# An attention and GEGLU kernel: first weights loaded by halves of their columns, and scores placed next to values in two chunks

## The chip, the cores and the metric

The kernel runs on one core of a Trainium2 chip. The metric is the device time of one execution in microseconds (us), median of several runs; "before" gave 348.88 us in three runs (348.76 to 349.36). The granted clock is the share of its full clock that TensorE was given; 0.50 is half clock. TensorE is PE in the profile, VectorE DVE, ScalarE ACT, GpSimd POOL, the queue of the sync engine SPq.

## The reference

```
batch, heads, seq, dim = 8, 8, 576, 64          # q, k, v float32
mask: heads 0-3: 0 <= i-j < 32;  heads 4-7: 0 <= i-j < 128 and (i-j) % 4 == 0
attn = softmax(q k^T / 8, masked);  x = attn v, reshaped to [4608, 512]
out  = (gelu(x @ w_gate) * (x @ w_val)) @ w_out  # w_gate, w_val [512,1536], w_out [1536,512]
```

## The kernel before

x is kept transposed in four slices of 128 features (`xT[0..3]`). The dense part runs in nine chunks of 512 tokens, each in 12 blocks of 128 hidden columns. A block is 4 gate and 4 value matmuls (one for each slice of xT), a Gelu on ScalarE and a product on VectorE. Four output blocks of 12 matmuls follow in each chunk, and the attention of later batches is put between these. The weights come in thirds of 512 hidden columns.

```
    def load_w(i):                                   # one third of both matrices
        cs = slice(i * CH, (i + 1) * CH)
        both = [nc.gpsimd.dma_start(out=t[i], in_=w[:, cs].rearrange("(kc p) n -> p kc n", p=P))
                for t, w in ((wg_t, moe_w_gate), (wv_t, moe_w_val))]
        gated(both[0])                               # waits for the load named in gate["dma"]
        return both
    ...
    gate["dma"] = gate_v                             # first piece of v of batch 0
    load_w(0)
    v_cast(0, sv0)
    ...
    w1 = load_w(1)[1]
    copy("pool", tiles["v", 0][1], r4(first_vd))     # cast of v, dilated heads
    ...                                              # attention of batch 0; xT[0], xT[1] finished
    load_w(2)                                        # on GpSimd, xT[2], xT[3] on VectorE
    gate["dma"] = w1                                 # q, k of batch 1 wait for the second third
    for t, src in ((0, q), (1, k)):
        gated(nc.sync.dma_start(out=st1[:, t], in_=sixes(src, 1)))
    qd1 = load_eights(1)
    wo1 = [load_wo(i) for i in range(3)][1]
    load_v_dil(1)
    ... cast_six("pool", q61, st1, t, hp)            # four casts, transposed by TensorE in block 10, 11
```

In chunk 0, blocks 0 and 1 are computed together, slice by slice (`ffn1_two`), so that TensorE can begin as soon as the first slice is ready. The places of the attention work are strings such as "3.6v": in output block 3 ahead of matmul 6, values. `s` is scores (TensorE, then the exponential on ScalarE), `v` values with their denominators, `x` the normalisation on VectorE, `m` the mask of an earlier score on VectorE, `w` the last values of the chunk, which use the scores' PSUM banks (pieces of `ps`, the memory into which the matmuls write). `P` is the exponentials.

The softmax here doesn't subtract the row's maximum and nothing guards it: scores larger than these inputs give would overflow.

Of the kernel before, what the change touches and what calls it, by code (L numbers as in the profile page):

```python
# [21 lines left out]
def kernel(  # L22
# [10 lines left out]
    nc = tc.nc  # L33
# [3 lines left out]
    P = 128  # L37
# [3 lines left out]
    CH = 512  # L41
# [31 lines left out]
    wg_t = [const.tile([P, NKC, CH], F16, tag=f"wg{i}", name=f"wg{i}") for i in range(3)]  # L73
    wv_t = [const.tile([P, NKC, CH], F16, tag=f"wv{i}", name=f"wv{i}") for i in range(3)]
# [61 lines left out]
    def load_w(i):  # L136
        cs = slice(i * CH, (i + 1) * CH)
        both = [
            nc.gpsimd.dma_start(out=t[i], in_=w[:, cs].rearrange("(kc p) n -> p kc n", p=P))
            for t, w in ((wg_t, moe_w_gate), (wv_t, moe_w_val))  # L140
        ]
        gated(both[0])
        return both

    def load_wo(i):
        return nc.gpsimd.dma_start(
            out=wo_t[i], in_=moe_w_out[i * CH : (i + 1) * CH, :].rearrange("(fc p) m -> p fc m", p=P)
        )
# [4 lines left out]
    def gated(ins):  # L153

        if "dma" in gate:
            tc.add_manual_dep(ins.ins, gate.pop("dma").ins.name, SYNC, reason="order of loads")
# [45 lines left out]
    def v_cast(b, sv):  # L202
        vp, vd, vt, vr = tiles["v", b]
        nc.gpsimd.tensor_copy(  # L204
            vp.rearrange("p j g x d -> p (j g) x d")[:, :, 0:3:2, :],
            sv[:, 0:4].rearrange("p j (g x) d -> p (j g) x d", x=2),
        )
        nc.gpsimd.tensor_copy(vt[:, :, 0:3:2, :], sv[:, 4].rearrange("p (g x) d -> p g x d", x=2))
# [468 lines left out]
        t_plain(0, q6, hp, 2 * hp, ("act", "dve"))  # L677
    nc.vector.tensor_scalar(bias_d, mask_d, 1.0, 60000.0, ALU.subtract, ALU.mult)
    gate["dma"] = gate_v
    load_w(0)  # L680
    v_cast(0, sv0)

    def r4(t):
# [21 lines left out]
    last_keys(0, 0, 2)  # L705
    last_keys(0, 2, HK, nc.gpsimd)
    w1 = load_w(1)[1]
    copy("pool", tiles["v", 0][1], r4(first_vd))

# [12 lines left out]


    load_w(2)
    gate["dma"] = w1
    st1 = ldp.tile([R6, 2, HK, 6 * D], F32, tag="st", name="st1")
# [8 lines left out]
    for hp in range(2):  # L735
# [16 lines left out]

    places = {
        1: "0.0m 1.3v 1.3s 1.3x 1.3m 2.5v 2.5s 2.5x 2.5m 3.0s 3.0m 3.6v 3.6x 3.12w",
        2: "0.0m 1.3v 1.3s 1.3x 1.3m 2.5v 2.5s 2.5x 2.5m 3.0s 3.0m 3.6v 3.6x 3.7s 3.12w 3.12m",
        3: "0.0m 1.3v 1.3s 1.3x 1.3m 2.5v 2.5s 2.5x 2.5m 2.11s 2.11m 3.4s 3.6v 3.6x 3.6m",
        4: "0.0m 1.3v 1.3s 1.3x 1.3m 2.4v 2.4s 2.4x 2.4m 2.11s 2.11m 3.7s 3.7m",
        5: "0.0m 1.3v 1.3s 1.3x 1.3m 2.1s 2.1m 2.10s 2.10m 3.6s 3.6m",
    }
# [2 lines left out]
    for c in range(NCH):  # L762
# [13 lines left out]
        for nb in range(NNB):  # L776
# [19 lines left out]
            if nb == NNB - 1 and c > 0 and s_list:  # L796
                n = s_list.pop(0)
# [130 lines left out]
```

## Time and profile before

| | before |
|---|---|
| time, median of 3 | 348.88 us |
| span of the profiled run | 347.3 us |
| TensorE busy | 335.7 us (97%) |
| VectorE, ScalarE, GpSimd busy | 58%, 43%, 24% |
| granted clock of TensorE | 1.00 |

A row of the order in time has the start, the length, the engine, the line and the operation, then in brackets the engine's idle time ahead of it and what ended that. A row of the chain has start, length and what the end of the kernel waited for at that time.

### The profile page before, as it was taken

To read this page: it belongs to the slowest core of one execution; us is meant where nothing else is said; L and a number is where in the kernel's file an instruction comes from. 1 tells how busy PE (TensorE), PEld (TensorE's weight loads), DVE (VectorE), ACT (ScalarE), POOL (GpSimd) and SP (SyncE) were. 2 spreads that over 40 slices of the span, in tenths; PEclk is the share of its full clock that TensorE was granted. 3 is DMA by queue.
4 is the path that set the end of the run, shared out by engine and by line. 5 is a ranking of instruction groups with operands and counts; after the bars stand their busy time and mean duration, and the time that the engine had idled before them with its cause. 6 is when DMAs were issued, how large, how long until landed. Compare 5 with 4: busy or idle time off the path is not lost.

```text
span 347.3 us, 6004 instructions
## 1 busy us (share of the span) xinstructions
PE 335.7 (97%) x2342; PEld 163.3 (47%) x2342; DVE 202.1 (58%) x309; ACT 147.9 (43%) x220; POOL 82.2 (24%) x121
## 2 busy tenths in 40 slices
PE   8879999999999999999999999999999999999996
PEld 3544454444544444444544454445444444444443
DVE  3874488543793369674778676975398423303320
ACT  1753473535543446336553547236623223323321
POOL 8693304630630630243006300420000000000000
PEclk9999999999999999999999999999999999999999
DMA  8999999999999993897169924891100020020002
GB/s 176 227 202 225 200 201 181 184 153 272 195 142 273 194 143 101 183 175 121 63 157 170 149 79 130 183 145 49 74 2 0 32 91 1 2 90 30 2 30 91
DMA packets 106460, 44.44 MB, mean 128 GB/s; under 512 B 83296, under 2 KB 101856, under 8 KB 106432
## 3 DMA queue, kind: packets, MB, share of 16 engines
q1 hardware_dynamic: 84192, 31.01, 40.7%
q0 software_dynamic: 21696, 12.33, 27.4%
q10 hardware_dynamic: 544, 0.72, 0.8%
q8 instruction: 18, 0.29, 0.4%
q14 instruction: 10, 0.08, 0.1%
HBM read 39.85 MB, written 9.44 MB: 142 GB/s over the span
## 4 chain that ended last, share of the span: by engine, by line
PE 71%; DVE 12%; DMA 10%; issue 3%; ACT 2%; POOL 1%; SPq 1%; DVEq 0%; POOLq 0%; ACTq 0%
PE ps L576 42%; PE ps L610 21%; PE ps L464 4%; DMA st<-in_k_dram 4%; DMA sv<-in_v_dram 3%; DMA wv<-in_moe_w_val_dram 3%; DVE dt L492 2%; DVE u_all L599 2%; DVE dt L525 2%; DVE rb L536 1%; DVE P L392 1%; DVE xT L551 1%; DVE xT L502 1%; PE ps L382 1%; PE ps L352 1%
## 5 line engine op out<-in xcount | busy, mean ns | idle before, releaser
L599 DVE SCALAR_TENSOR_TENSOR u_all<-g,ps 128x512 f16<-128x512 f16 x108 | 72.8, 684 | 76.3 <-PE ps L576 67.9
L598 ACT ACTIVATE g<-ps 128x512 f16<-128x512 f32 x108 | 63.9, 596 | 123.4 <-PE ps L576 122.9
L576 PE MATMUL ps<-xT,wg 128*128 128x512 f16 x432 | 114.0, 379 | 0.8 <-POOL xT L699 0.4
L576 PE MATMUL ps<-xT,wv 128*128 128x512 f16 x432 | 113.8, 379 | 0.8 <-DMA wv<-in_moe_w_val_dram 0.6
L610 PE MATMUL ps<-wo,u_all 128*128 128x512 f16 x420 | 97.2, 380 | 0.2 <-DVE qTd L295 0.2
L576 PEld LDWEIGHTS <-wv 128*128 128x128 f16 x432 | 42.3, 98 | 53.0 <-issue 1.6
L576 PEld LDWEIGHTS <-wg 128*128 128x128 f16 x432 | 41.3, 98 | 48.7 <-issue 1.1
L610 PEld LDWEIGHTS <-u_all 128*128 128x128 f16 x420 | 38.4, 98 | 44.4 <-issue 0.8
L621 ACT ACTIVATE osb<-ps 128x512 f32<-128x512 f32 x33 | 19.7, 598 | 40.0 <-PE ps L610 39.9
L220 POOL CAST qp<-st 128x2048 f16<-128x2048 f32 x6 | 11.4, 1893 | 103.5 <-DMA sv<-in_v_dram 59.0
L536 DVE STREAM_TRANSPOSE rb<-rc 128x576 f32<-128x576 f32 (+4 forms) x34 | 25.3, 743 | 1.3
L525 DVE STREAM_TRANSPOSE dt<-ps 128x576 f32<-128x576 f32 x21 | 16.3, 778 | 13.2 <-PE ps L464 13.0
L384 ACT ACTIVATE P<-ps 128x1152 f16<-128x1152 f32 x16 | 18.1, 1130 | 12.0 <-PE ps L382 12.0
L362 ACT ACTIVATE P<-ps 128x960 f16<-128x960 f32 x16 | 15.5, 970 | 10.4 <-PE ps L352 10.3
L551 DVE TENSOR_TENSOR xT<-ps,rb 128x576 f16<-128x576 f32 x16 | 17.9, 1131 | 2.2 <-PE ps L464 1.9
L392 DVE TENSOR_TENSOR P<-P,mask_d 128x1152 f16<-128x1152 f16 x13 | 9.8, 750 | 9.7 <-ACT P L384 9.7
L392 DVE TENSOR_TENSOR P<-P,mask_p 128x1344 f16<-128x1344 f16 x14 | 11.8, 856 | 2.9 <-ACT P L363 2.9
L464 PE MATMUL ps<-P,ones 128*64 128x96 f16 (+5 forms) x174 | 11.2, 244 | 2.2 <-DVE P L392 1.5
L464 PEld LDWEIGHTS <-ones 128*64 128x64 f16 x174 | 7.0, 109 | 11.6 <-issue 8.8
L623 DVE TENSOR_SCALAR osb<-ps 128x512 f32<-128x512 f32 x2 | 1.4, 691 | 18.2 <-PE ps L610 18.2
L204 POOL CAST vp<-sv 128x1024 f16<-128x1024 f32 x8 | 8.5, 1065 | 12.8 <-DMA sv<-in_v_dram 12.8
L492 DVE STREAM_TRANSPOSE dt<-ps 64x576 f32<-64x576 f32 x14 | 10.9, 781 | 0.4
(86 smaller groups left out, 247.0 us busy)
## 6 DMA issues: line engine op xcount, KB each, us to landing
out_dram<-osb SPq DMA_DIRECT2D x35, 256.0 KB, 2.0
sv<-in_v_dram SPq DMA_DIRECT2D x40, 128.0 KB, 3.5
st<-in_q_dram SPq DMA_DIRECT2D x24, 128.0 KB, 3.0
st<-in_k_dram SPq DMA_DIRECT2D x24, 128.0 KB, 3.7
vd<-in_v_dram POOLq DMA_DIRECT2D x7, 256.0 KB, 6.3
wg<-in_moe_w_gate_dram POOLq DMA_DIRECT2D x3, 512.0 KB, 7.4
wv<-in_moe_w_val_dram POOLq DMA_DIRECT2D x3, 512.0 KB, 10.3
wo<-in_moe_w_out_dram POOLq DMA_DIRECT2D x3, 512.0 KB, 20.0
```

What stands on the lines that cost most here:

```text
L384: nc.scalar.activation(pt, ps[:, b0 : b0 + 4, 0:DW], AF.Exp, bias=0.0, scale=scale)
L392: nc.vector.tensor_tensor(pt, pt, mb, ALU.mult)
L464: nc.tensor.matmul(o, lhs, rhs, start=st, stop=True, skip_group_check=True)
L492: nc.vector.transpose(dt[64 * hl : 64 * hl + 64].rearrange("p b c -> p (b c)"), both_rows(1 - hl, b0, hl))
L525: nc.vector.transpose(dst, den)
L536: nc.vector.transpose(rb[:, 0 : 32 * nb].rearrange("p (b c) -> p b c", c=32), bass.AP(tensor=rc.tensor, offset=rc.offset, ap=[rc.ap[0], [1 ...
L551: nc.vector.tensor_tensor(dst.rearrange("p (i m s) -> p i m s", m=2, s=2), num, rb.rearrange("p (s m i) -> p i m s", s=2, m=2), ALU.mult,)
L576: nc.tensor.matmul(ps[:, bank, :], w[:, kc, ns], xT[kc][:, tok], start=first, stop=end)
L598: nc.scalar.activation(g, ps[:, banks[0], :], AF.Gelu)
L599: nc.vector.scalar_tensor_tensor(u_all[:, nb, :], g, USCALE, ps[:, banks[1], :], ALU.mult, ALU.mult)
L610: nc.tensor.matmul(ps[:, bank, :], u_all[:, fc, tb * P : (tb + 1) * P], wo_t[fc // 4][:, fc % 4, :], start=(fc == 0), stop=(fc == NNB - 1),)
L621: nc.scalar.activation(osb, ps[:, bank, :], AF.Copy, bias=0.0, scale=1.0 / USCALE)
```

## The change

Its intent is twofold. TensorE waits for the first value weights at 21.2 us, while only the columns of blocks 0 and 1 are needed by then; halves, taken by turns, bring these sooner. And in chunks 2 and 3 one group of scores is moved directly behind a group of values, which saves a switch of the array's tiling.

```
+    def load_w_halves(i):
+        for half in range(2):
+            cs = slice(half * CH // 2, (half + 1) * CH // 2)
+            for t, w in ((wg_t, moe_w_gate), (wv_t, moe_w_val)):
+                src = w[:, i * CH : (i + 1) * CH][:, cs].rearrange("(kc p) n -> p kc n", p=P)
+                gated(nc.gpsimd.dma_start(out=t[i][:, :, cs], in_=src))
...
-    load_w(0)
+    load_w_halves(0)
...
-        2: "... 3.0s 3.0m 3.6v 3.6x 3.7s 3.12w 3.12m",
-        3: "... 2.11s 2.11m 3.4s 3.6v 3.6x 3.6m",
+        2: "... 3.0s 3.0m 3.6v 3.6s 3.6x 3.12w 3.12m",
+        3: "... 2.11s 2.11m 3.6v 3.6s 3.6x 3.6m",
```

## The prediction

> **What bounds the kernel now.** I read the page of the kernel before from its top: busy shares, then the chain of work that ended last, then the waits, and at last the order in time of the two stretches that the change touches.
>
> ```profile
> PE 335.7 (97%) x2342; PEld 163.3 (47%) x2342; DVE 202.1 (58%) x309; ACT 147.9 (43%) x220; POOL 82.2 (24%) x121
> ...
> PE ps L576 42%; PE ps L610 21%; PE ps L464 4%; DMA st<-in_k_dram 4%; DMA sv<-in_v_dram 3%; DMA wv<-in_moe_w_val_dram 3%; DVE dt L492 2%; DVE u_all L599 2%; DVE dt L525 2%; DVE rb L536 1%; DVE P L392 1%; DVE xT L551 1%; DVE xT L502 1%; PE ps L382 1%; PE ps L352 1%
> ```
>
> TensorE is busy 335.7 of 347.3 us, so only 11.6 us of its idle time exist to be won, and no single change of order can be worth per cents. But the chain also names three transfers: `sv` (v of the first batch), `wv` (value weights) and `st` (k of the second batch). In order of time, for the first 60 us, the chain reads:
>
> ```profile
> 3.70 11.39 DMA sv<-in_v_dram
> ...
> 16.98 0.68 POOL wg L139
> 17.65 9.21 DMA wv<-in_moe_w_val_dram
> ...
> 27.30 13.19 DMA st<-in_k_dram
> ...
> 40.54 0.83 POOL qp L293
> ```
>
> So up to 41.4 us the chain is a queue of loads: the second third of the weights (issued at 16.98) lands at 26.86, that landing lets the k of batch 1 be issued at 27.30, it lands at 40.48, GpSimd casts it, and only then can TensorE transpose it. The first third, which the change splits, travels on the same transfer engines ahead of that second third.
>
> TensorE's side of the start, from its order in time (start, length, then the idle time before and its releaser in brackets):
>
> ```profile
> 20.87 0.38 PE L576 MATMUL ps<-xT,wg 128*128 128x512 f16 x1 [0.37 <-POOL xT L699]
> 21.84 0.39 PE L576 MATMUL ps<-xT,wv 128*128 128x512 f16 x1 [0.59 <-DMA wv<-in_moe_w_val_dram]
> ...
> 24.34 0.38 PE L576 MATMUL ps<-xT,wg 128*128 128x512 f16 x1
> ...
> 41.42 0.43 PE L306 MATMUL ps<-ident,qp 96*128 96x96 f16 x6 [0.26 <-POOL qp L293]
> ```
>
> The 0.59 us is the wait that the halves are to remove. Two later lines matter more: at 24.34 TensorE has just been let go by VectorE's last normalisation (`norm_x`, two L551 instructions from 22.17 for 2.12 us, so to 24.29), and at 41.42 it waits for GpSimd's cast of the late k.
>
> The end of chunks 2 and 3:
>
> ```profile
> 133.24 0.49 PE L464 MATMUL ps<-P,ones 128*64 128x64 f16 x10 [0.22 <-DVE P L392]
> ...
> 134.28 0.47 PE L352 MATMUL ps<-qTp 64*128 64x160 f16 x10
> ...
> 136.18 0.49 PE L464 MATMUL ps<-P,ones 128*64 128x64 f16 x10 [0.25 <-ACT P L363]
> ...
> 171.08 0.77 PE L352 MATMUL ps<-qTp 64*128 64x160 f16 x10
> ```
>
> In chunk 2 the last values of the chunk (136.18) wait for the exponentials of scores issued at 134.28, because they reuse those PSUM banks. In chunk 3 the scores at 171.08 take 0.70 us until the next start where others take 0.40: ScalarE's previous exponential on the same banks ends only at 171.34.
>
> **What the Trainium skill says.** "DMA: Bandwidth & Descriptors", section "Why small descriptors are slow (HBM only)", gives every packet a fixed overhead and every transfer operation fixed metadata, so smaller pieces cost more per byte. The trace agrees: its records of single packets show weight packets of 1024 B taking 98 ns, and packets of 512 B (the later loads of q and k, `qd`, 256 values a row, the same shape as a half) taking 60 ns. Two of these for one of those is 120 against 98, 22% more. The same page, "Issuing engines are not separate DMA queues", says that loads from different engines end up on the same 16 transfer engines and interleave; the trace agrees, as the k load's packets and the weights' run mixed from 30 to 39 us, the weights' queue falling from about 200 packets a us to about 80. "TensorEngine Tiling (Array Packing)", section "Key Properties", says that changing the tiling mode drains TensorE. In the trace 14 full matmuls before a switch to values take 3.12 us (88.06 to 91.18), 14 x 0.216 = 3.02, so a switch out of full tiles costs 0.10; values followed directly by scores cost nothing extra (123.87 to 124.51 is 0.64; values followed by full matmuls, 172.31 to 172.96, 0.65).
>
> **Part 1, the halves.** No arithmetic changes and the bytes are the same. GpSimd issues four loads in place of two, 2 x 0.77 = 1.54 us more. From 12.29 to 15.25 it idles for `sv` (2.96 us), so these are hidden. First the gain: both first halves together are 1024 packets of 512 B; they should land by about 19.5 us, and columns 0 to 255 are all that blocks 0 and 1 read. So at 20.87 TensorE goes on to the value weights at once, and the 0.59 us vanish. But then the second slice of xT is ready only at about 22.17 (GpSimd, 19.39 + 2.78), the third at 23.24, the fourth at 24.29 (VectorE). TensorE is at 24.34 for the fourth slice in both kernels. Worth: about 0. Neither engine's chain starts from the weights.
>
> Now the cost. The first third is 2 x 128 x 4 = 1024 packets of 1024 B, in the halves 2048 of 512 B. Where only such packets run, the trace counts about 202 a us of 1024 B, and 308 to 310 a us of 512 B in the microseconds at 75 and 102, with 30 to 63 small ones beside; allowing for those, 325. That is 1024/202 = 5.1 us against 2048/325 = 6.3 us: **1.2 us more**. GpSimd's queue carries packets without a pause from 14 us to beyond 45 us, so everything behind moves by 1.2 us: the second third's landing from 26.86 to about 28.1, the issue of batch 1's q and k behind it, k's landing from 40.48 to about 41.7, the cast to 42.5, and the transposes that started at 41.42 to about 42.6. TensorE arrives there at 41.16 as before, so the whole 1.2 us is idle time on the path. The loads behind it (output weights, v of batch 1) move by the same 1.2 us as TensorE, so they neither help nor hurt. Part 1: **+1.2 us**.
>
> **Part 2, chunk 2.** The scores move ahead of one output matmul and adjoin the values, which end at 133.94. They start there in place of 134.28: one switch (0.10) and one matmul (0.22) earlier, so the exponentials end at 135.8 in place of 136.13. TensorE, with six output matmuls after the scores, arrives at 135.74; the last values start at 135.84 in place of 136.18. VectorE idles 0.34 us before its transposes at 137.09, so it can follow. **-0.34 us**.
>
> **Part 3, chunk 3.** The scores move behind the values, so they no longer meet the busy banks (0.30 saved) and one switch goes (0.10). But the values then arrive at 169.89 + 7 x 0.216 + 0.10 = 171.50, and their P is masked by VectorE only at 171.63 (0.75 from 170.88), so they start at 171.70: 0.20 lost again. Then 0.65 values, 0.40 scores, 6 x 0.216 = 1.30: the next chunk starts at 174.05 in place of 174.26. The exponentials now end at about 174.2 in place of 173.21; the first matmul of chunk 4 needs only the banks of the first exponential (free at 173.7), and the second group, at 174.70, those of the second. No new wait. **-0.21 us**.
>
> Sum: 1.2 - 0.34 - 0.21 = +0.65, so 348.88 + 0.65 = 349.5.
>
> **The rivals.** (a) The transfers do not delay anything: 512 B packets mixed with others flow as well per byte as 1024 B ones. Then only parts 2 and 3 count, 348.3. For it: the packets' 60 ns is a duration with overlap, not a rate. Against: the counted rates show the same ratio. (b) The halves bring the intended 0.59 us as well: 347.7. Against: xT sets 24.34, and k sets 41.42, where any earlier arrival would only wait. (c) In chunk 3 ScalarE becomes the bound: its exponentials, now 1 us later, hold the banks of chunk 4's first matmuls, up to 0.6 us, so 350.1. Against: by the sums above 0.3 to 0.5 us remain. (d) `sv` gains from smaller weight packets beside it and GpSimd starts earlier: useless for the same reason as (b).
>
> **Range and chances.** I believe the transfer argument most, about two in three; rival (a) or something half-way about one in four. Weighted, I put 349.3 rather than 349.5. The range 348.1 to 350.2 takes in rival (a) and most of (c). Two per cent is 7 us, more than half of all idle time of TensorE, so within 2% is nearly certain.
>
> **What would show it right or wrong.** Right for part 1: no wait of TensorE on `wv` at 21 us, yet the fourth slice still at about 24.3; packets of 512 B in the weights' time; `st` of k landing near 41.7; TensorE idle about 1.4 us before the transposes at about 42.6. If k lands near 40.5 again, the step of 1.2 us has failed. For part 2: the wait on ACT before the chunk's last values falls from 0.25 to 0.1 or less. For part 3: a wait of about 0.2 us on VectorE's mask before the third values of chunk 3, scores of 0.40 us right behind, and no wait on ACT at the start of chunk 4. A slow state of the chip, or a wait in chunks 0 and 1 that absorbs the delay, would make the sum wrong though the steps hold.

## The result, and the profile after

The changed kernel took 348.65 us (median of 4, 348.54 to 349.01), against 349.02 us for the kernel before in the same rounds (348.76 to 349.36). The ratio is 0.9991 with a 95% interval of 0.9973 to 1.0008. Ratios here are the mean time of one kernel's fast runs over that of the other's of the same rounds, so not quite the ratio of the medians. By the times alone the change is nothing that can be told from zero. The traces say more, since their events can be laid side by side. (Lines of the changed kernel have numbers 8 higher.)

| event, us from the span's start | before | after | difference |
|---|---|---|---|
| first value matmul of block 0 | 21.84 | 21.18 | -0.66 |
| matmuls on the fourth slice of xT | 24.34 | 24.43 | +0.09 |
| k of batch 1 has landed | 40.49 | 40.64 | +0.15 |
| its transposes on TensorE | 41.42 | 41.57 | +0.15 |
| last values of chunk 2 | 136.18 | 136.02 | -0.16 |
| first matmul of chunk 4 | 174.26 | 173.90 | -0.36 |
| span | 347.3 | 347.0 | -0.3 |

So the first stretch, up to the transposes of k, is 0.15 us longer in this pair of traces (k's landing alone varies by more than that from run to run, as shown below); chunk 2 wins 0.15 + 0.16 = 0.31 us, chunk 3 a further 0.36 - 0.16 = 0.20.

The start of the dense part in the changed kernel, TensorE in order of time:

```profile
20.97 0.38 PE L584 MATMUL ps<-xT,wg 128*128 128x512 f16 x1 [0.37 <-POOL xT L707]
21.18 0.38 PE L584 MATMUL ps<-xT,wv 128*128 128x512 f16 x1
...
22.32 0.38 PE L584 MATMUL ps<-xT,wg 128*128 128x512 f16 x1 [0.33 <-POOL xT L707]
...
24.43 0.38 PE L584 MATMUL ps<-xT,wg 128*128 128x512 f16 x1
...
41.57 0.43 PE L314 MATMUL ps<-ident,qp 96*128 96x96 f16 x6 [0.32 <-POOL qp L301]
```

The reader is to see that the wait for `wv` has gone, that a wait for the second slice of xT (0.33 us at 22.32) has come, and that the fourth slice is started no earlier than before. At the transposes the wait for GpSimd's cast of k is still there. The chain of waits gives the loads behind it:

```profile
17.74 9.37 DMA wv<-in_moe_w_val_dram
...
27.55 13.09 DMA st<-in_k_dram
...
40.69 0.83 POOL qp L301
```

These are the three rows that the prediction shows for the kernel before. The second third lands at 27.11 in place of 26.86, k at 40.64 in place of 40.49. The 1.2 us of the prediction are not there.

The ends of chunks 2 and 3:

```profile
133.40 0.49 PE L472 MATMUL ps<-P,ones 128*64 128x64 f16 x10 [0.22 <-DVE P L400]
...
134.11 0.47 PE L360 MATMUL ps<-qTp 64*128 64x160 f16 x10
134.51 1.47 PE L618 MATMUL ps<-wo,u_all 128*128 128x512 f16 x6
136.02 0.49 PE L472 MATMUL ps<-P,ones 128*64 128x64 f16 x10
...
171.52 0.47 PE L472 MATMUL ps<-P,ones 128*64 128x192 f16 x8
...
172.20 0.47 PE L360 MATMUL ps<-qTp 64*128 64x160 f16 x10
172.60 1.47 PE L618 MATMUL ps<-wo,u_all 128*128 128x512 f16 x6
173.90 0.81 PE L584 MATMUL ps<-xT,wg 128*128 128x512 f16 x3
```

The scores (64x160) now stand right behind the values in both chunks. The last values of chunk 2 no longer carry a wait on ACT (0.25 us before), and in chunk 3 the scores take 0.40 us until the next start in place of 0.70.

### The profile page after: what moved, and what is told of

Same layout as the page of the kernel before. It is cut to its first block, busy times and chain, and to the rows that moved or that the text cites. A ratio compares the mean times of both kernels' runs of the same rounds, so it can differ in the third digit from the quotient of the medians.

```text
span 347.0 us, 6006 instructions
## 1 busy us (share of the span) xinstructions
PE 336.0 (97%) x2342; PEld 163.7 (47%) x2342; DVE 201.8 (58%) x309; ACT 148.2 (43%) x220; POOL 84.0 (24%) x123
## 3 DMA queue, kind: packets, MB, share of 16 engines
q1 hardware_dynamic: 84192, 31.01, 39.2%
## 4 chain that ended last, share of the span: by engine, by line
PE 70%; DVE 13%; DMA 10%; issue 3%; ACT 2%; SPq 1%; POOL 1%; DVEq 0%; POOLq 0%; ACTq 0%
PE ps L584 42%; PE ps L618 21%; PE ps L472 4%; DMA st<-in_k_dram 4%; DMA sv<-in_v_dram 3%; DMA wv<-in_moe_w_val_dram 3%; DVE dt L500 2%; DVE dt L533 2%; DVE u_all L607 2%; DVE xT L559 2%; DVE rb L544 2%; DVE P L400 2%; DVE xT L510 1%; PE ps L390 1%; DVE rc L542 1%
## 5 line engine op out<-in xcount | busy, mean ns | idle before, releaser
L255 POOL DMA_DIRECT2D vr<-in_v_dram x16 | 9.9, 632 | 5.3 <-DMA wv<-in_moe_w_val_dram 3.6
```

## The experiments

Eleven kernels were run. All gave correct results. The question was first why the transfers did not delay k, then why TensorE's earlier start at 21 us brings nothing, and last whether something better follows.

### Part 1 alone, and parts 2 and 3 alone

The edits are the change's own: `halves_only` keeps the new load and the old strings of places, `places_only` the old load and the new strings.

> Part 1 alone, the order of the chunks as before. Theory N (formed after the result): the weights' 512 B packets, alone on the engines, pass at about 370 a us, nearly as fast per byte as those of 1024 B (202 a us), so k of batch 1 lands 0.1 to 0.3 us later than in the kernel before (40.5), the transposes start at about 41.6, and the time is +0.1 us (0 to 0.3). Theory O (the prediction's step): 1.2 us more of transfer, k at 41.7, time +1.2 us, and the changed order hid it. Theory G: the vanished wait of 0.59 us pays, time -0.3 to -0.6 us.

> Parts 2 and 3 alone, loads as before. Theory N: the whole gain is here: the last values of chunk 2 start 0.32 us earlier against the transposes of batch 1 than in the kernel before, chunk 4 a further 0.20 us, time -0.5 us. Theory G: nothing of it is here, the time is that of before within 0.1 us.

Measured, in the same rounds (before 348.90 us, 9 runs): `halves_only` 349.05 us, ratio 1.0004 (0.9991 to 1.0016); `places_only` 348.47 us, ratio 0.9985 (0.9972 to 0.9997). This is theory N: part 1 is worth +0.1 us and can't be told from zero, parts 2 and 3 together -0.5 us. In the trace of `halves_only`, TensorE came to the transposes earlier than in the kernel before, and only waited longer there:

```profile
24.18 0.38 PE L584 MATMUL ps<-xT,wg 128*128 128x512 f16 x1
...
41.57 0.43 PE L314 MATMUL ps<-ident,qp 96*128 96x96 f16 x6 [0.57 <-POOL qp L301]
```

The fourth slice came 0.16 us sooner in this run, the wait for k grew from 0.26 to 0.57 us, and the transposes started at 41.57 as in the changed kernel. A loss of 1.2 us is excluded by the interval (1.2 us would be a ratio of 1.0034), and the trace shows none. In `places_only` the last values of chunk 2 start 94.44 us after the transposes of k (135.91 - 41.47), in the kernel before 94.76 (136.18 - 41.42), so 0.32 us are won there; the start of chunk 4 then comes 37.89 us after those values in place of 38.08, 0.19 us more.

### How fast do small packets go?

Two more kernels load the first third by quarters (packets of 256 B), or the second third by halves as well.

```
 quarters:   for part in range(4): cs = slice(part * CH // 4, (part + 1) * CH // 4) ...
 w1_halves:  -    w1 = load_w(1)[1]
             +    w1 = load_w_halves(1)        # returns its last load
```

> The changed kernel with the first third in quarters of its columns: 4096 packets of 256 B, to see whether transfer time ahead of k really reaches k and TensorE. Theory N: packets of 256 B last 40 ns where those of 512 B last 60; at the same overlap 560 pass in a us, so 7.3 us against 5.5, k lands about 1.8 us later than in the changed kernel (42.4 to 42.6) and the first transposes of it start at about 43.3, TensorE loses about 1.7 us. GpSimd's four more issues (3.1 us against 1.36 us of its idle time) bring the first projection 1.7 us later, about 22.7, which the later k hides. Rival: transfers ahead of k do not matter, since another thing (such as the landing order on the slowest engine) sets k: k stays at 40.6 to 41.0, and only GpSimd's delay shows, TensorE at the transposes about 1.2 us later.

> The changed kernel with the second third by halves too, the load of batch 1 released by the last of its four. Theory N: 0.4 us more transfer, the second third lands at 27.3 to 27.6 and k at 40.9 to 41.2 (from 40.6). Theory O: 1.2 us more per third: k at 41.8 or later. GpSimd's two more issues (1.5 us) delay the cast of v and the first slices of xT: the first projection at about 22.5 in place of 20.97, so TensorE reaches the transposes about 1.2 us later and the time is up to +1.1 us on the changed kernel, whichever theory holds; the landing is what tells them apart.

The trace records every packet of the transfer engines. Counted by the microsecond, on GpSimd's queue:

```
us from start         14   15   16   17   18   19   20   21   22   23
before     1024 B     26  115  181  187  201  192  203  203  197  204
changed     512 B     59  232  373  360  374  367  240   43
           1024 B                            10   76  183  198  203
quarters    256 B    172  441  684  663  694  677  516  239
w1_halves   512 B     94  260  384  361  377  381  388  380  383  383
```

By the end of microsecond 21 the kernel before has moved 1308 packets of 1024 B, the changed one 1024 + 269 = 1293 in the same measure. The difference is 15 packets, under 0.1 us. But one pair is not enough. Counted the same way in ten traces (all but `quarters`, `w1_halves` and `loads_late_split`, whose loads up to here differ), the five kernels with whole thirds had moved 1308 to 1399 packets (mean 1352) and the five with the halves 1282 to 1309 (mean 1297): 54 packets, or about 0.3 us, is the better estimate of what the halves cost in transfer. With the queue full, the rates are about 202, 380 and 690 packets a us, that is 207, 195 and 177 kB a us: halving the packet costs 6% more time per byte and quartering it 17%, where the prediction had 22 to 24% for halving. At 690 a us the quarters need 4096/690 = 5.9 us, against 1024/202 = 5.1.

Theory N's rate of 560 for the quarters was too low too: it came again from packet durations. In `quarters` k's first cast begins at 40.86, in `w1_halves` at 41.32 (40.69 in the changed kernel). Theory O's 1.2 us or more is not there, but finer than that the cast can't be read: in `s_before_v`, which has the changed kernel's loads, it begins at 41.41. The times, 350.70 us (ratio 1.0049, 1.0034 to 1.0064) and 349.93 us (1.0030, 1.0016 to 1.0043), are longer, at least in part, for the other reason that was foreseen, GpSimd's issues. Its queue in `quarters`:

```profile
15.30 0.80 POOL L151 DMA_DIRECT2D wg<-in_moe_w_gate_dram  x1
16.03 0.81 POOL L151 DMA_DIRECT2D wv<-in_moe_w_val_dram  x1
16.76 1.11 POOL L212 CAST vp<-sv 128x1024 f16<-128x1024 f32 x1
```

The cast of v, which stands at 15.34 in the changed kernel, comes at 16.76, since each issue holds GpSimd for about 0.77 us. The quarters delayed the packets behind them by about 0.6 us (1172 packets by the end of microsecond 21, against a mean of 1297 with halves), no more than k's landing varies by itself. So this run had no lever on the second question, whether packets ahead of k matter to k at all. It stayed open.

Both runs show an addition to such a loss. In `w1_halves` TensorE waited 1.54 us for the delayed cast of v, in `quarters` 1.70 us for a delayed copy of keys, and then each ran 3.4 us at half clock, from 20.85 and 18.98. How much of the longer times this makes was not separated. The rows are stretches of 2 us: length, then the busy time of PE, PEld, DVE, ACT and POOL with their instructions, the granted clock, the DMA share and GB/s. Two of `w1_halves`, then one of `quarters`:

```profile
20.00:22.00 2.00, 1.31 (x26) 1.20 (x28) 0.23 (x2) 1.13 (x1) 2.00 (x3) 0.71 1.45 197
22.00:24.00 2.00, 2.00 (x15) 0.81 (x10) 1.86 (x4) 0.00 (x0) 2.00 (x2) 0.50 1.46 196
...
20.00:22.00 2.00, 1.75 (x28) 1.46 (x27) 1.42 (x3) 1.74 (x4) 2.00 (x2) 0.50 1.47 172
```

### Fewer packets beside k, and what the halves are worth then

Three kernels move the loads that run beside k: the strided q and k of batch 1 (`qd`) behind the casts of q, the output weights and v behind the casts of k. `loads_late` is built on the changed kernel, `loads_late_whole` on `places_only`; `loads_late_split` also moves the value half of the second third behind GpSimd's two normalisations.

```
-    qd1 = load_eights(1)
-    wo1 = [load_wo(i) for i in range(3)][1]
-    load_v_dil(1)
     q61 = ...
     for hp in range(2): cast_six("pool", q61, st1, 0, hp)
+    qd1 = load_eights(1)
     for hp in range(2): cast_six("pool", q61, st1, 1, hp)
-    gate["dma"] = wo1
+    wo0 = [load_wo(i) for i in range(3)][0]
+    load_v_dil(1)
+    gate["dma"] = wo0
```

> The changed kernel with the second batch's strided q and k (qd) issued after the casts of q, the output weights and v (vd, vr) after the casts of k, v_plain released by the first output weights: fewer packets beside batch 1's k. Theory: k lands at 37.5 to 39 in place of 40.6, TensorE no longer waits for its cast at the transposes (0.32 us in the changed kernel), time -0.3 to -0.4 us on the changed kernel if no later load then holds TensorE. Rival: the k load is slow for its own reasons, not for the packets beside it: k stays at about 40.5, no gain. Second rival: the output weights, now first issued at about 40, hold the first output block (46.3), a loss of some tenths.

> The same move of the late loads, but with the first third loaded whole as in the kernel before (order of chunks as changed). It tells what the halves are worth once k no longer holds TensorE. Theory X: the fourth slice of xT still sets the start of block 0's last matmuls (24.1 to 24.4 in both), so the halves are worth 0 to 0.1 us even here: same time as loads_late within 0.15 us. Theory K: only the late k had hidden the gain, so this one is 0.3 to 0.6 us slower than loads_late.

> loads_late, and besides on GpSimd's queue the value half of the second third is issued behind the two normalisations in place of ahead of the cast of v: xT's chain starts 0.4 us earlier. Theory X: the cast of v starts at about 17.8, TensorE does not wait 0.44 us for it, VectorE's last slice is ready at about 23.9 and the last matmuls of block 0 start at about 24.0 in place of 24.4; with k out of the way 0.3 to 0.4 us faster than loads_late. Rival: the value weights of block 4 (needed at 29.4) or a wait on ScalarE's copy takes its place, no gain.

Measured (before 349.17 us): 353.46, 352.49 and 353.89 us, ratios 1.0121, 1.0104 and 1.0137. All three lose more than 1%, in the way of the second rival, though it had forecast only some tenths of a microsecond. GpSimd and TensorE in `loads_late`:

```profile
37.65 1.60 POOL L301 CAST qp<-st 96x768 f16<-96x768 f32 x2
...
40.63 0.68 PE L314 MATMUL ps<-ident,qp 96*128 96x96 f16 x12
...
46.79 1.02 PE L618 MATMUL ps<-wo,u_all 128*128 128x512 f16 x4 [1.42 <-DMA wo<-in_moe_w_out_dram]
...
58.75 0.45 PE L472 MATMUL ps<-P,vp 128*64 128x160 f16 x8 [2.72 <-POOL vp L212]
```

The casts of k run at 37.65 without a wait for the load, 3 us sooner than in the changed kernel. k's load took 9.5 us from issue to landing in place of 13.1, so packets beside k do matter to k. TensorE does all 12 transposes at 40.63 without waiting. Then the output weights hold it for 1.42 us and v of batch 1 for 2.72 us, and after the second wait its clock is halved for 3.4 us. The gain was turned into two later waits.

In the stage where k no longer waits, before those later waits, the two loads of the first third can be compared: the transposes start at 40.63 with halves and at 40.55 with the whole third. This favours theory X, though the times of these two kernels, disturbed by the later waits (`loads_late_whole` also ran at half clock, from 48.6 to 52.0), are no use for it. `loads_late_split` is inconclusive for its own question: its clock was halved from 15.3 to 18.7 us, ScalarE's copies came late (the first normalisation at 20.37 waited 1.44 us for them), and the first projection started at 21.82, 1.06 us later than in `loads_late`. It waited 2.87 us for the output weights and had a second stretch at half clock, from 49.4.

### Releasing k a little sooner

These keep the order of all loads and only release q and k of batch 1 by the Gelu of block 1, which ends at about 25.9, in place of the landing of the second third at 27.1.

```
-    gate["dma"] = w1
+    gate["dma"] = last_g[-1]      # the block of loads is now emitted behind block 1's Gelu
```

`k_sooner` has the halves, `k_sooner_whole` does not, both have the new places. `k_sooner_s3` is described below.

> The changed kernel with batch 1's q and k released by block 1's Gelu (ends at about 25.9) in place of the landing of the second third (27.1): the same loads in the same order, q and k 1.2 us sooner. Theory: k lands at 39.2 to 39.7, its cast ends before TensorE comes at 41.2, the wait at the transposes (0.3 to 0.9 us by run) goes, time -0.3 to -0.6 us on the changed kernel. Rival: the last third's value half, now beside q and k for longer, lands after 36.3 and holds block 8, which eats the gain.

> The same release with the first third loaded whole (order of chunks as changed): are the halves worth anything where k comes in time and no later load is moved? Theory X: the slices of xT set the start of block 0's last matmuls at 24.1 to 24.4 with either load, so equal to k_sooner within 0.15 us, though TensorE waits 0.5 us for the value weights at about 21.3. Theory K: 0.3 to 0.6 us slower than k_sooner.

Measured (before 348.82 us): `k_sooner` 347.87 us, ratio 0.9966 (0.9953 to 0.9978); `k_sooner_whole` 348.02 us, ratio 0.9976 (0.9960 to 0.9991). The spans of the profiled runs are 346.2 and 346.0 us. The wait at the transposes has gone in both. In `k_sooner`:

```profile
22.05 2.13 DVE L560 TENSOR_TENSOR xT<-ps,rb 128x576 f16<-128x576 f32 x2
...
24.23 0.38 PE L585 MATMUL ps<-xT,wg 128*128 128x512 f16 x1
...
40.63 0.68 PE L315 MATMUL ps<-ident,qp 96*128 96x96 f16 x12
```

And in `k_sooner_whole`, with its wait for the value weights:

```profile
21.60 0.39 PE L577 MATMUL ps<-xT,wv 128*128 128x512 f16 x1 [0.61 <-DMA wv<-in_moe_w_val_dram]
...
21.82 2.12 DVE L552 TENSOR_TENSOR xT<-ps,rb 128x576 f16<-128x576 f32 x2
...
23.99 0.38 PE L577 MATMUL ps<-xT,wg 128*128 128x512 f16 x1
...
40.39 0.68 PE L307 MATMUL ps<-ident,qp 96*128 96x96 f16 x12
```

With the whole third TensorE waits 0.61 us at 21.60, yet comes to the fourth slice at 23.99 and to the transposes at 40.39, no later than with halves (24.23 and 40.63). So a late k was not what hid a gain of the halves: the fourth slice of xT takes it up. The DVE row of each is VectorE's normalisation of the third and fourth slice; it ends at 24.18 and 23.94, and TensorE starts on the fourth slice 0.05 us after that in both. In the same ten traces as were counted above, this distance is 0.05 or 0.06 us, but for `loads_late_whole`, where TensorE had waited 0.82 us for the value weights and came 0.16 us after. So the halves are worth 0 to 0.1 us here. The end of the normalisation itself lay between 24.12 and 24.55 with halves and between 23.87 and 24.29 with the whole third; whether the halves delay it was not tested. The intervals of the two ratios overlap and don't exclude a few tenths of a microsecond either way.

`k_sooner` gained more than was forecast: 0.8 us by the spans against the changed kernel, not 0.3 to 0.6, though k landed at 39.9, a little later than the 39.2 to 39.7 expected. From the first transpose to the next gate matmul it takes 0.51 us (40.63 to 41.14) where the changed kernel takes 1.01 (40.83 to 41.84), so the wait that the profile showed as 0.32 us cost 0.50. Another 0.2 us is an earlier xT (24.23 for 24.43), which is not the release's doing as far as the traces show.

k itself landed anywhere from 40.5 to 41.4 us across traces of the old release (40.49 before, 40.64 after, 41.36 in `s_before_v`, whose program is that of the changed kernel up to chunk 2). Whether waiting on such an event spreads the times is not shown: the five runs of `k_sooner` lie within 0.13 us and the eleven of the kernel before within 1.26, but the six of `k_sooner_whole`, which does not wait for k either, within 1.19.

### Scores ahead of the values

```
-  2: "... 3.6v 3.6s 3.6x 3.12w 3.12m",   3: "... 3.6v 3.6s 3.6x 3.6m",
+  2: "... 3.6s 3.6v 3.6x 3.12w 3.12m",   3: "... 3.6s 3.6v 3.6x 3.6m",
```

> The changed kernel with scores ahead of the values at the same place in chunks 2 and 3 (v waits 0.2 us for VectorE's mask there; scores could fill that wait). Theory: in chunk 3 0.1 to 0.2 us are won, as VectorE has slack there; in chunk 2 the last values start 0.2 us earlier but VectorE's chain then starts 0.2 us later and holds the first blocks of chunk 3, so nothing or a loss of 0.1 to 0.2 us; in all within 0.15 us of the changed kernel. Rival (adjoining with scores behind is what pays): 0.2 us or more slower than the changed kernel.

Measured: 348.78 us, ratio 0.9989 (0.9973 to 1.0005), as the changed kernel's 0.9991 within the intervals. In the trace chunk 3 goes as expected: from the seven output matmuls to the next chunk 3.96 us (170.62 to 174.58) in place of 4.17. In chunk 2 the same stretch to the last values is 0.22 us shorter (4.09 in place of 4.31), but from the same start to the value matmuls of block 2 in chunk 3, which wait for VectorE's product, it takes 10.19 us in place of 10.00. The row of `s_before_v`, then that of the changed kernel:

```profile
142.60 1.02 PE L584 MATMUL ps<-xT,wv 128*128 128x512 f16 x4 [0.34 <-DVE u_all L607]
...
141.71 1.02 PE L584 MATMUL ps<-xT,wv 128*128 128x512 f16 x4 [0.23 <-DVE u_all L607]
```

So in chunk 2 scores first lose 0.19 us, more than they had won, and chunk 3's 0.21 us only makes that good: from the start of the stretch in chunk 2 to chunk 4 it takes 42.17 us in place of 42.19. So the last kernel puts scores first in chunk 3 alone, on `k_sooner_whole`:

> Candidate for the best: k_sooner_whole and besides, in chunk 3 alone, scores ahead of the values, so that the wait for VectorE's mask (0.2 us) is filled. Theory: the stretch from the end of the scores at fc 11 to the next chunk falls from 4.17 us to 3.96, as in the run with scores ahead in both chunks, without that run's later wait in chunk 3's first blocks: 0.2 us faster than k_sooner_whole, 0.8 to 1.2 us faster than the kernel before, that is a ratio of 0.9965 to 0.998.

Measured: 347.75 us, ratio 0.9961 (0.9949 to 0.9973). In its trace:

```profile
168.72 1.68 PE L611 MATMUL ps<-wo,u_all 128*128 128x512 f16 x7
170.33 0.47 PE L353 MATMUL ps<-qTp 64*128 64x160 f16 x10
...
172.68 0.81 PE L577 MATMUL ps<-xT,wg 128*128 128x512 f16 x3
```

The stretch is 3.96 us as wanted. This is the fastest version, 1.07 us below the kernel before by medians of the same rounds and probably faster than the changed kernel, whose interval against before includes 1 (the two were measured in different calls). The ratio is a little better than the 0.9965 to 0.998 forecast. The 0.2 us that it should have over `k_sooner_whole` are within the intervals and are shown by the trace alone.

## Why the prediction was right or wrong

The time is inside the range (348.1 to 350.2), but it moved the other way from the middle of the forecast: 0.3 us faster by the spans, where the prediction had 0.4 us slower. It lies inside only because the range was drawn to take in rival (a), which stands at 348.3; that is no credit to the main line of the argument. One step of five failed.

- **The gain of the halves, "Worth: about 0": right.** The 0.59 us of waiting vanished and a wait for the second slice of xT took its place; the fourth slice came no sooner (24.34 and 24.43). (The first halves were there earlier than "about 19.5": by the counts their 1024 packets had passed at 18.0. It changes nothing, as TensorE comes at 21.) `loads_late` against `loads_late_whole` and `k_sooner` against `k_sooner_whole` show the same with k out of the way.
- **The cost of the halves, "1.2 us more": wrong, and this is the failed step.** The term was 2048/325 - 1024/202; the 325 packets a us were mis-sized. They had been counted in whole microseconds in which packets of the other queue ran beside them or the queue was not full all the time. The trace of the kernel before itself has half-microseconds with next to nothing else on the engines, those from 159.5 and 161.0 us, where 512 B packets pass at 388 and 392 a us; 2048/388 = 5.3 us would have given +0.2. Measured: 0.3 us more transfer by the packets counted in ten traces, +0.15 us at k's landing in the one pair, +0.1 us in the times of `halves_only` (-0.3 to +0.6 by its interval). The supporting figure of 98 and 60 ns was one of durations that overlap, which the prediction itself remarked under its rival (a). That rival was nearly right: half packets cost 6%, not nothing. Why those loads of q and k ran slower in the counted microseconds was not tried.
- **The path from the loads to TensorE**: right as far as it was tested. Packets beside k delay k (`loads_late`, casts 3 us sooner without them), an earlier release brings k sooner, and k's cast holds the transposes (`k_sooner`). That a delay of the first third would reach k in full, as the sum assumed, stays untested: no run delayed it by more than k's own spread.
- **Chunk 2, -0.34 us: right.** 0.31 us in the changed kernel, 0.32 in `places_only`.
- **Chunk 3, -0.21 us: right.** 0.20 and 0.19 us. The values started at 171.52 behind VectorE's mask, and no wait on ScalarE came at the start of chunk 4, so rival (c) falls.

Summed with the measured term, 0.15 - 0.31 - 0.20 = -0.36 us, which is the table's row for chunk 4 again; the spans agree within their rounding.

## What to carry to other kernels

A rate of the transfer engines is to be counted where their queue is full and nothing else runs, not from a packet's duration nor from a mixed microsecond. A wait that the profile names is worth something only if the next operand is also there in time: look one and two waits further down the same engine. And where the wait is on a load, first ask what releases it; here a release about 1.2 us earlier won 0.3 and 0.9 us by the ratios of the two pairs of kernels, more than all reshaping of the loads, and moving loads out of its way lost more than it won.

## What the Trainium skill lacked or had wrong

- "DMA: Bandwidth & Descriptors", section "Why small descriptors are slow (HBM only)": its fixed cost for each packet is right in kind, but it gives no rate for loads that cast from float32 to float16. The runs show, with a full queue, about 202, 380 and 690 packets a us for 1024, 512 and 256 B written, that is 207, 195 and 177 kB a us.
- No page gives the time that GpSimd is held by issuing such a load. It was about 0.77 us for each load (0.74 to 0.81), nearly the same for rows of 512, 256 or 128 columns; in `quarters`, with four issues more than the changed kernel, the cast of v moved from 15.3 to 16.8 us.
- "TensorE: Matmul & The Clock Gate", section "What's actually happening", has the clock fall after an idle window of some 3.4 us. In these runs a window need not be idle throughout. Within each run the changes of clock lie whole multiples of 3.41 us apart. In the 3.41 us ahead of a stretch at half clock TensorE was idle, by the trace, for 2.05 us (`quarters`), 2.10 (`w1_halves`), 2.61 (`loads_late`), 1.81 (`loads_late_whole`), and 1.22 and 2.86 (`loads_late_split`); windows (stretches of 3.41 us counted from a run's first change of clock) that no fall followed had up to 1.56 (the kernel before). The length of a single wait does not decide: 2.00 us in `loads_late_whole`, from 57.36 and so spread over two windows, was not followed by half clock. That it is the idle time within one window that counts is an inference, and the 1.22 does not fit it.
- "TensorEngine Tiling (Array Packing)", section "Key Properties", says that a change of tiling drains TensorE but not what that costs. Here a switch out of full tiles cost 0.10 us, one from values to scores nothing that shows.
